# The mLSTM cell and leaky-ReLU feed-forward kernel: a written order for the first chunk and w_in in five requests per quarter

## The chip, the cores and the metric

The kernel runs on one core of a Trainium2 chip. The core has a matrix engine (TensorE, "PE" in the profile, with "PEld" for its weight loads), VectorE (DVE), ScalarE (ACT), GpSimd (POOL) and SyncE (SP), each with an instruction queue of its own, and 16 DMA engines that move data between HBM and the on-chip memory of 128 partitions. Most transfers are issued from SP's queue (SPq), a few from ScalarE's (ACTq). The metric is the device time of one execution in microseconds (us); less is better. One further execution was taken with the hardware profiler.

## What is computed

Four sequences, eight heads, 768 tokens, head dimension 40 go through an mLSTM cell; the result, 3,072 tokens by 320, goes through a two-layer feed-forward block with 2,048 hidden units:

```python
for t in range(S):
    m_new = np.maximum(f_gate[:, :, t] + m, i_gate[:, :, t])
    f_stab = np.exp(f_gate[:, :, t] + m - m_new)
    i_stab = np.exp(i_gate[:, :, t] - m_new)
    C = f_stab * C + i_stab * outer(v[t], k[t])        # per batch and head, 40 x 40
    n = f_stab * n + i_stab * k[t]
    y[t] = sigmoid(o_gate[t]) * (C @ q[t]) / max(|n . q[t]|, 1)
x = y.transpose(0, 2, 1, 3).reshape(B * S, H * D)      # 3072 x 320
h = x @ w_in                                           # w_in is 320 x 2048
out = np.maximum(0.01 * h, h) @ w_out                  # w_out is 2048 x 320
```

q, k, v and the gates arrive as 32-bit floats. The two weight matrices arrive as 64-bit floats, 5.2 MB each, and are narrowed to 32 bits on the chip.

## The kernel before, in words

The 768 tokens are cut into six chunks of 128. One *step* is one chunk of one sequence, so there are 24 steps, four to a chunk, numbered s = 4 x chunk + sequence. The recurrence is computed in the parallel form: scores of k and q, a decay matrix, and a state carried from one half chunk of 64 tokens to the next. One *group* g of the feed-forward block takes the four steps of chunk g: 512 tokens.

Up to the end of group 0 everything is issued by `first_chunk`, which walks through a text called ORDER. Each entry is a short name with numbers and calls one function. For TensorE, VectorE, ScalarE and GpSimd that text is the order in the engine's queue (`manual_schedule`); in the kernel before, SP is not among these engines, and its requests are placed by the scheduler. After it, a planned loop handles groups 1 to 5 with the remaining steps woven in.

The entries that matter here:

- `ld s i`, `lo s`: load k, q or v (i = 0, 1, 2) of a step of chunk 0, or its o gate; 128 partitions, eight rows of 160 bytes each. `fd s` loads k and v of a later step and spreads its gate decays over the partitions. `fi c` loads the gates of chunk c.
- `lw n half`: one half of quarter n of w_in (n below 4), or w_out piece n - 4 (two blocks of 128 rows). It lands in a raw 64-bit area.
- `nw n`: one of seven steps of narrowing. The first is on ScalarE (L263), six more on VectorE (L265 to L280). They need the whole of quarter n.
- `ff n`: unit n of group 0. Units 0 to 15 compute h for half of the tokens and two blocks of 128 hidden units (L918, 20 matmul instructions), and end in the leaky ReLU on ScalarE (L926); units 4 to 7 need quarter 1, 8 to 11 quarter 2, 12 to 15 quarter 3. Units 16 to 31 are the product with w_out (L953).
- `us`, `qs`, `tq`: transposes of k and q of a step of chunk 1 on TensorE. `qs` scales q by its decay, and `tq` (split_qs, L562 and L564) transposes the scaled q: 16 matmuls of 64 rows by 40 columns, into two banks, and two copies to SBUF on ScalarE.
- `up`, `upl`, `ux`: scores and states of a step of chunk 1, its outputs, and the transposes that make its x. `st`, `stc`: the first states, from chunk 0.

Partition p of either half of w_in holds the five rows 5p to 5p + 4. The lower 64 partitions (r = 0) hold 256 columns of the quarter, and the upper 64 (r = 1) the next 256. TensorE uses the two halves of its rows at the same time. A quarter comes in two requests, one for each half of the partitions (L231 to L235). The functions that the change touches, and what calls them:

Of the kernel before, what the change touches and what calls it, by code (L numbers as in the profile page):

```python
# [22 lines left out]
def kernel(  # L23
# [56 lines left out]
    psc = ctx.enter_context(tc.tile_pool(name="psc", bufs=4, space=PSUM))  # L80
# [5 lines left out]

    RG = P // BH
# [4 lines left out]
    for r in range(RG):  # L92
        nc.scalar.dma_start(f0[ts(r, BH), :], f_all[:, :P])
        nc.sync.dma_start(i0[ts(r, BH), :], i_all[:, :P])
    fi = {}

    def load_fi(c):
        t = fi[c] = wk.tile([BH, 2, P], F32, name="fi")
        eng = nc.scalar if c < 3 else nc.sync
        eng.dma_start(t[:, 0, :], f_all[:, ts(c, P)])  # L100
        eng.dma_start(t[:, 1, :], i_all[:, ts(c, P)])

    load_fi(1)
    load_fi(2)

    ident = consts.tile([P, P], F32, name="ident")
    make_identity(nc, ident[:])
    zeros = consts.tile([P, 1], F32, name="zeros")
    nc.vector.memset(zeros[:], 0.0)
# [3 lines left out]
    nc.gpsimd.memset(cmask[:], 0.0)  # L113
    nc.gpsimd.affine_select(
        cmask[:], cmask[:], compare_op=ALU.is_ge, fill=-1e30,
        base=0, pattern=[[1, P]], channel_multiplier=-1,
    )
    ident_b = consts.tile([P, P], BF16, name="ident_b")
    nc.vector.tensor_copy(ident_b[:], ident[:])
# [16 lines left out]
    for n in range(NL):  # L136
        nc.vector.memset(kn[:, n, :, D:], 0.0)
        nc.vector.memset(qn[:, n, :, D:], 0.0)
        nc.gpsimd.memset(S_t[n][:, 1, :, D:], 2.0)
        nc.gpsimd.memset(S_t[n][SL:, 0], 0.0)  # L140
# [66 lines left out]
    def load_weights(n, half=None):  # L207
# [22 lines left out]
        if n < QN:  # L230
            src = moe_w_in[:, n * QC : (n + 1) * QC].rearrange("(p k) (r c) -> r p k c", p=DP, r=2)  # L231
            for r in range(2) if half is None else (half,):
                nc.sync.dma_start(
                    to[DP * r : DP * (r + 1), :].rearrange("p (k c) -> p k c", k=KC), src[r],
                )  # L235
        else:
            rows = moe_w_out[2 * m * P : 2 * (m + 1) * P, :]
            nc.sync.dma_start(to.rearrange("p (a d) -> p a d", d=Dm), rows.rearrange("(a p) d -> p a d", p=P))
# [102 lines left out]
    def gates_T(c, bu):  # L341
        tg = psc.tile([P, 5, BH], F32, name="tg", tag="c")
# [18 lines left out]
    def load(s, i=None):  # L361
# [5 lines left out]
        if c == 0:  # L367
            d["va"] = S_t[n][:, 1]
            parts = [(d["k"][:, :, :D], k), (d["q"][:, :, :D], q), (d["va"][:, :, :D], v)]
            for dst, src in parts if i is None else parts[i : i + 1]:  # L370
                nc.sync.dma_start(dst, src[b, :, rows, :].rearrange("h p d -> p h d"))
            return
        nc.sync.dma_start(d["k"][:, :, :D], k[b, :, rows, :].rearrange("h p d -> p h d"))
        w = cw.tile([P, H, P], F32, name="w", bufs=NL)
        flat = w[:].rearrange("p h t -> p (h t)")
        d["w"] = flat[:, : H * SL].rearrange("p (h t) -> p h t", t=SL)
        if c == 1:
            for u in range(2):
                for i in range(2):
                    nc.sync.dma_start(  # L380
                        S_v[n][ts(u, SL), u, :, i, :DB],
                        v[b, :, c * P + u * SL : c * P + (u + 1) * SL, DB * i : DB * (i + 1)].rearrange("h p d -> p h d"),
                    )
            return
        d["vn"] = flat[:, H * SL : H * (SL + D)].rearrange("p (h d) -> p h d", d=D)
        nc.sync.dma_start(d["vn"], v[b, :, rows, :].rearrange("h p d -> p h d"))
# [9 lines left out]
    def load_o(s, eng=None):  # L396
# [3 lines left out]
        (eng or nc.sync).dma_start(  # L400
# [8 lines left out]
    def load_late(s, i):  # L409

        if B <= s < 2 * B:
            if i > 0:
                c, b = divmod(s, B)
                nc.sync.dma_start(natural(s, i), (k, q, o_gate)[i][b, :, ts(c, P), :].rearrange("h p d -> p h d"))
        elif s < NS:
            load_blocks(s, i)

    def load_blocks(s, i):
# [3 lines left out]
        for n in range(2):  # L422
            for r in range(2):
# [6 lines left out]
                nc.sync.dma_start(  # L430
# [7 lines left out]
    def spread(s):  # L438
# [3 lines left out]
        for u in range(2):  # L442
            nc.sync.dma_start(d["w"][ts(u, SL)], a_dr[c, 0, u, b * H : (b + 1) * H, :].partition_broadcast(SL))

    def spread_q(s):
# [4 lines left out]
        for r in range(2):  # L450
            nc.sync.dma_start(
# [23 lines left out]
    def exp_first(s, g):  # L475

        ab, n = st["ab", s - s % 2], s % 2
        if g == 0:
            st[s]["w"] = cw.tile([P, H, P], F32, name="w", bufs=NL)
# [77 lines left out]
    def split_qs(s):  # L557

        tq = [psc.tile([P, H, SL], F32, name=f"tq{u}", tag="c") for u in range(2)]
        for h in range(H):  # L560
            for u, toks, rows in subs(s):
                nc.tensor.matmul(tq[u][rows, h, :], lhsT=st[s]["qs"][toks, h], rhs=ident[toks, toks], start=True, stop=True)  # L562
        for u, toks, rows in subs(s):
            nc.scalar.copy(mixed(s)[rows, u], tq[u][rows])  # L564

    def u_split(s):
# [4 lines left out]
        bank = [psc.tile([P, H, SL], F32, name=f"tk{r}", tag="c") for r in range(2)]  # L571
# [12 lines left out]
    def u_transpose(s, i):  # L584
# [3 lines left out]
        tp = d["tp", i] = psc.tile([P, PR, P], F32, name="tkq", tag="c")  # L588
# [10 lines left out]
    def u_scores(s):  # L599
        d = st[s]  # L600
        kqT = d["kqT"]
        sc = d["sc"] = [psc.tile([P, PR, P], F32, name=f"sc{r}", tag="c") for r in range(2)]
# [12 lines left out]
    def state(s):  # L615
        c, b = divmod(s, B)
        d = st[s]
        dC = d["dC"] = psc.tile([P, PR, 2, V1], F32, name="dC", tag="c")
# [28 lines left out]
    def u_parts(s):  # L647
# [4 lines left out]
        bank = [psc.tile([P, H, SL], F32, name=f"sd{r}", tag="c") for r in range(2)]  # L652
# [27 lines left out]
    def u_values(s):  # L680
        d = st[s]
        pa = d["pa"] = psc.tile([P, H, D1], F32, name="pa", tag="c")
# [32 lines left out]
    def u_plain(s):  # L715
# [4 lines left out]
        hN = psc.tile([P, H, 2, V1], F32, name="hN", tag="c")  # L720
# [22 lines left out]
    def u_mix(s):  # L743
# [4 lines left out]
        pT = psc.tile([P, PR * P], F32, name="pT", tag="c")  # L748
# [27 lines left out]
    def gather_x(s):  # L776
# [6 lines left out]
        for r in range(2):  # L783
            nc.sync.dma_start(xT[DP * r : DP * (r + 1), b, :], src)
# [49 lines left out]
    def three_units(g, lead):  # L834
# [14 lines left out]
        def triple(j):  # L849
# [9 lines left out]
            def third():  # L859
                pe.extend(psc.tile([P, GT], F32, name=f"pe{r}", tag="c") for r in range(2))  # L860
# [20 lines left out]
    def u_x(s):  # L881
# [3 lines left out]
        xt = st["xt", s] = psc.tile([P, KF + 1, P], F32, name="xt", tag="c")  # L885
# [199 lines left out]

    ORDER = """
warm 12; g 0; ld 0 0; mk 0; ab 0; ge 0; ld 0 1; ld 1 0; lo 1; ld 0 2; ld 1 1; ld 2 0; ug 0; exp 0 0
ld 1 2; exp 1 0; exp 1 2; exp 0 2; exp 0 3; tr 0 0; tc 0 0 0; tr 0 1; exp 0 1; tr 1 0; tc 0 1 0
exp 1 3; ld 2 1; tr 1 1; sc 0; lw 0 0; scm 0 0; lw 0 1; tc 1 0 0; scm 0 1; mk 2; ab 2; lo 0; tc 1 1 0
ld 3 0; g 1; ld 3 1; ld 3 2; sc 1; exp 1 1; scm 1 1; ld 2 2; exp 2 0; tr 2 0; tr 2 1; tc 2 1 0; lw 1 0  # L1090
lw 1 1; vu 0; exp 2 2; val 0; fi 3; exp 3 0; lo 2; exp 3 2; st 0; scm 1 0; stc 0 0 0; exp 2 3
stc 0 1 0; den 0; exp 2 1; lo 3; tc 2 0 1; sc 2; o 1; lw 2 0; o 0; scm 2 0; gate 0; gp 0; ge 1
scm 2 1; nw 0; val 1; den 1; x 0; xc 0 1; gate 1; tr 3 0; tr 3 1; tc 3 1 1; nw 0; nw 0; gp 1; x 1
tc 3 0 0; sc 3; xc 1 1; vu 3; nw 0; nw 0; st 3; vu 2; vu 1; val 2; exp 3 1; exp 3 3; stc 3 1 1; st 2
stc 2 1 1; scm 3 1; scm 3 0; val 3; nw 0; tiles; ps 3; stc 2 0 1; stc 3 0 1; nw 0; o 2; den 2; den 3
gate 2; o 3; gate 3; nw 1; st 1; nw 1; nw 1; ug 1; ff 0; gp 2; x 2; xc 2 1; gp 3; nw 1; nw 1; x 3
xc 3 1; ff 1; nw 1; ff 2; nw 1; ps 0; g 2; lw 2 1; nw 2; ff 3; lw 3 0; lw 3 1; ps 2; ff 4; ff 5; nw 2
nw 2; ff 6; nw 2; ff 7; fd 4; lw 4; lw 5; stc 1 0 1; ps 1; vu 4; nw 2; nw 2; nw 2; nw 3; nw 3; nw 3
nw 3; nw 3; nw 3; nw 3; nw 4; ff 8; ff 9; ff 10; nw 4; ff 11; ff 12; nw 4; nw 4; ff 13; nw 4; nw 4
nw 4; stc 1 1 0; pm 4; sn 4 0; fd 5; ll 5 1; nw 5; ll 4 1; us 4; lw 6; lw 7; fd 6; lz 6; vu 6; fd 7  # L1100
qs 5; qs 4; pm 6; us 5; lw 8; nw 5; nw 5; nw 5; nw 5; nw 5; ff 14; pm 5; nw 5; ll 5 2; lw 9; nw 6
nw 6; lz 7; nw 6; lz 4; ex 4 3; nw 6; ff 15; ll 6 0; ex 4 3; ex 4 2; nw 6; ll 4 2; nw 6; ge 2; nw 6
pm 7; nw 7; ex 6 3; ex 6 3; tq 4; sn 5 0; nw 7; ll 7 0; ll 7 1; vu 5; up 4; nw 7; ff 16; ff 17; ex 7 3
ff 18; ff 19; nw 7; ll 8 0; nw 7; nw 7; nw 7; nw 8; nw 8; nw 8; nw 8; ug2 2; nw 8; nw 8; tq 5; upl 4
lw 10; nw 8; vu 7; ll 6 1; nw 9; nw 9; nw 9; lw 11; lz 5; fd 8; ex 7 3; nw 9; ll 9 0; nw 9; ex 5 3
nw 9; sn 6 0; nw 9; ex 5 3; ff 20; nw 10; nw 10; qs 6; ex 5 2; up 5; us 7; qs 7; nw 10; nw 10; ff 21
sn 7 0; ff 22; ux 4; upl 5; ll 9 1; nw 10; nw 10; nw 10; nw 11; nw 11; nw 11; ex 6 2; ff 23; pv 8
sq 9; nw 11; ll 7 2; nw 11; tq 7; us 6; ll 8 1; pm 8; lz 8; ex 8 3; tq 6; ff 24; nw 11; nw 11; xb0
ll 6 2; up 6; ex 7 2; up 7; ff 25; upl 6; fd 9; sn 9 0; upl 7; kq 9; fd 10; pv 9; sq 8; ll 8 2; pm 9
kq 8; ll 11 1; sq 11; fd 11; ll 10 1; sn 8 0; ll 9 2; ex 8 3; ll 11 0; lz 9; vu 8; vu 9; ff 26; ff 27  # L1110
ff 28; ff 29; ux 5; ux 6; ux 7; sq 10; ff 30; ex 8 2; ff 31; ex 9 3; ex 9 3; ll 10 0; ex 9 2
"""

    def first_chunk():

        ffs, narrow = [], {}

# [167 lines left out]
```

## Time and profile before

| | us |
|---|---|
| median of three runs | 491.97 |
| the three runs | 485.73, 491.97, 492.03 |
| the profiled execution | 488.21 |
| its span, first to last instruction | 486.4 |
| TensorE busy | 476.2 (98%) |
| VectorE busy | 357.5 (73%) |
| ScalarE busy | 194.8 (40%) |
| GpSimd busy | 158.6 (33%) |
| mean granted TensorE clock | 0.988 |
| data moved | 63.41 MB in 142,187 packets |

The page cuts the span into 40 slices of 12.2 us; a digit is the busy share in tenths. TensorE shows 8 or 9 everywhere, and DMA 7 to 9 in the first nine slices and 5 or more in most of the next fifteen. A busy TensorE is not one at its peak. The first 133 us are the first chunk; the rest is the loop. In the answers of the trace a line of the timeline is start, duration, engine, line, operation, output and inputs, count, and in brackets how long the engine was idle before it and what ended that.

### The profile page before, as it was taken

How to read it: one execution, taken by the hardware profiler on the slowest of the kernel's cores; microseconds unless marked ns; L12 is line 12 of the kernel's file. 1: busy time of each engine (PE TensorE's matmuls, PEld its weight loads, DVE VectorE, ACT ScalarE, POOL GpSimd, SP SyncE). 2: the span in 40 equal slices, each digit the busy share in tenths (PEclk: the TensorE clock that was granted, in tenths of full speed). 3: DMA queues.
4: the chain of work that ended last, by engine and by line, in shares of the span. 5: the costliest groups of instructions: out<-in, count | busy, mean ns of one | idle time of the engine just before them, and what ended most of it. 6: DMA issues, size and time to landing. Idle time of an engine off the chain costs nothing.

```text
span 486.4 us, 12790 instructions
## 1 busy us (share of the span) xinstructions
PE 476.2 (98%) x5145; PEld 378.6 (78%) x5145; DVE 357.5 (73%) x581; ACT 194.8 (40%) x509; POOL 158.6 (33%) x207
## 2 busy tenths in 40 slices
PE   8899999899999999999999999999999999999997
PEld 7788887677746489965559985558998899988997
DVE  3887788978926999677898878679899968335611
ACT  3766549554442240414251131425024642156310
POOL 4074342443401816636370654544210002000020
PEclk9979999999999999999999999999999999999999
DMA  8999878775545577776776767754151030100001
GB/s 147 194 206 164 210 180 207 166 167 114 143 138 100 143 158 215 170 179 162 156 190 183 173 156 185 192 135 139 43 230 42 1 108 1 42 16 1 0 1 55
DMA packets 142187, 63.41 MB, mean 130 GB/s; under 512 B 110320, under 2 KB 130352, under 8 KB 142128
## 3 DMA queue, kind: packets, MB, share of 16 engines
q1 hardware_dynamic: 141744, 62.47, 54.3%
q8 instruction: 40, 0.66, 0.5%
q10 hardware_dynamic: 384, 0.13, 0.1%
q14 instruction: 19, 0.16, 0.1%
HBM read 51.68 MB, written 8.27 MB: 123 GB/s over the span
## 4 chain that ended last, share of the span: by engine, by line
PE 90%; DVE 3%; ACT 3%; issue 1%; POOL 1%; POOLq 0%; DVEq 0%
PE po L994 32%; PE ph L918 28%; PE ph L844 8%; PE po L953 5%; PE pe L844 4%; PE pT L754 3%; PE sd L661 3%; PE warm L339 1%; PE pa L684 1%; PE sd L666 1%; ACT w L483 1%; DVE qn L671 1%; PE hN L724 1%; PE tk L576 1%; ACT kqT L582 1%
## 5 line engine op out<-in xcount | busy, mean ns | idle before, releaser
L918 PE MATMUL ph<-xT,w_in 64*128 64x512 f32 (+1 forms) x800 | 144.0, 513 | 0.1
L918 PEld LDWEIGHTS ph<-xT,w_in 64*128 64x128 f32 x800 | 77.9, 190 | 56.7 <-issue 51.3
L994 PE MATMUL po<-w_out,acts 128*128 128x160 f32 x640 | 91.0, 301 | 0.0
L994 PEld LDWEIGHTS po<-w_out,acts 128*128 128x128 f32 x640 | 87.5, 190 | 3.4 <-ACT w L500 1.5
L926 ACT ACTIVATE acts<-ph 128x512 f32<-128x512 f32 (+1 forms) x80 | 37.4, 508 | 89.6 <-PE ph L918 89.1
L641 POOL TENSOR_TENSOR S<-S,f 40x336 f32<-40x336 f32 x36 | 32.5, 903 | 83.4 <-PE pT L754 53.1
L500 ACT ACTIVATE w<-w,gT 128x64 f32<-128x64 f32 x160 | 41.7, 339 | 27.8 <-POOL w L492 27.8
L994 PE MATMUL po<-raw,acts 128*128 128x160 f32 x320 | 45.1, 300 | 0.0
L994 PEld LDWEIGHTS po<-raw,acts 128*128 128x128 f32 x320 | 44.0, 190 | 0.0
L1027 POOL TENSOR_TENSOR y<-y,raw 128x160 f32<-128x160 f32 x10 | 5.5, 555 | 112.0 <-ACT y L1026 112.0
L671 DVE TENSOR_TENSOR qn<-w,sd 64x512 f32<-64x512 f32 x40 | 27.3, 683 | 18.6 <-PE sd L666 12.1
L953 PE MATMUL po<-w_out,acts 128*128 128x320 f32 x128 | 38.2, 454 | 0.0
L866 DVE SCALAR_TENSOR_TENSOR acts<-ph,acts 128x512 f32<-128x512 f32 x32 | 20.6, 685 | 20.6 <-ACT acts L864 20.6
L492 POOL TENSOR_TENSOR w<-w,i 128x512 f32<-128x512 f32 x20 | 32.8, 1644 | 6.9 <-DMA w<-a_dr 3.6
L553 DVE TENSOR_TENSOR qn<-kqT,late 64x512 f32<-64x512 f32 x32 | 34.0, 1062 | 1.0
L953 PEld LDWEIGHTS po<-w_out,acts 128*128 128x128 f32 x128 | 24.7, 198 | 10.0 <-issue 1.2
L768 POOL TENSOR_TENSOR xb<-xb,den 128x320 f32<-128x320 f32 x16 | 11.6, 727 | 48.9 <-DVE xb L765 48.9
L864 ACT ACTIVATE acts<-pe 128x512 f32<-128x512 f32 x32 | 17.4, 594 | 19.1 <-PE pe L844 19.0
L772 DVE STREAM_TRANSPOSE x<-xb 128x512 f32<-128x512 f32 x16 | 17.7, 1107 | 8.0 <-POOL xb L768 8.0
L661 PEld LDWEIGHTS sd<-kqT 40*64 40x64 f32 x640 | 19.6, 135 | 4.6 <-issue 4.2
L870 ACT ACTIVATE acts<-acts 128x512 f32<-128x512 f32 x32 | 19.7, 633 | 8.0 <-DVE acts L866 8.0
L994 PE MATMUL po<-raw 128*128 128x160 f32 x160 | 22.7, 300 | 0.0
(171 smaller groups left out, 768.0 us busy)
## 6 DMA issues: line engine op xcount, KB each, us to landing
w<-a_dr SPq DMA_DIRECT2D x40, 128.0 KB, 3.6
rb<-in_k_dram SPq DMA_DIRECT2D x64, 80.0 KB, 2.7
rb<-in_q_dram SPq DMA_DIRECT2D x64, 80.0 KB, 2.5
rb<-in_o_gate_dram SPq DMA_DIRECT2D x64, 80.0 KB, 2.4
xT<-x_dr SPq DMA_DIRECT2D x32, 160.0 KB, 3.2
late<-a_dr SPq DMA_DIRECT2D x32, 128.0 KB, 3.2
x_dr<-x SPq DMA_DIRECT2D x16, 256.0 KB, 2.8
kn<-in_k_dram SPq DMA_DIRECT2D x24, 160.0 KB, 4.1
```

The costliest lines, as they stand in the source:

```text
L492: nc.gpsimd.tensor_tensor(w, w, cm2.unsqueeze(1).to_broadcast([P, H, SL]), op=ALU.add)
L500: yield nc.scalar.activation(w[:, h, :], w[:, h, :], AF.Exp, bias=gT[c][:, 0, bh : bh + 1], scale=1.0)
L553: nc.vector.tensor_tensor(mixed(s)[rows, 1 - r], d["kqT"][rows, 1].rearrange("p (h t) -> p h t", t=SL), d["ea"][rows], op=ALU.mult,)
L641: nc.gpsimd.tensor_tensor(new, old, g, op=ALU.mult)
L661: nc.tensor.matmul(bank[1 - u][toks, h, :], lhsT=kqT[rows, 0, ts(h, SL)], rhs=kqT[rows, 1, ts(h, SL)], start=True, stop=True,)
L671: nc.vector.tensor_tensor(mixed(s)[toks, u], w[toks], bank[1 - u][toks], op=ALU.mult)
L844: nc.tensor.matmul(ph[r][:], lhsT=parts["w", key][n][part, at : at + P], rhs=xs[key][part, slot, :], start=start and slot == 0, stop=stop ...
L866: nc.vector.scalar_tensor_tensor(fs[r], in0=ph[r][:], scalar=1.0 + EPS, in1=fs[r], op0=ALU.mult, op1=ALU.add,)
L918: nc.tensor.matmul(ph[r][:, cols], lhsT=w_row(r, slot, j), rhs=xT[DP * r : DP * (r + 1), slot, bs, :], start=(slot == 0), stop=(slot == KC ...
L926: nc.scalar.activation(acts[:, f, cols], ph[r][:, cols], AF.Prelu, alpha=0.01)
L953: nc.tensor.matmul(po[n][:], lhsT=acts[:, f, ts(n, P)], rhs=w_out[:, f, :], start=(f == 0), stop=(f == NF - 1),)
L994: nc.tensor.matmul(bank[:], lhsT=left[:, f, :], rhs=right[:, f, :], start=f == 0, stop=f == KH - 1)
```

## The change

Four things are changed, all of them up to the end of the first chunk.

1. ORDER is another text, and SP is now among the engines whose queue follows it. The set-up work (gate loads, identity, masks, memsets) has become entries of it, and each load names its queue with a last number (1: ScalarE's, 0: SP's). `fd` is split into `fk`, `fv` and `fs`, and `lv` loads a piece of w_out.
2. The four rotating PSUM banks of the first chunk become four banks by number, dealt out in the order of a string, BANKS; the loop opens a rotating pool of four as before.
3. `split_qs` transposes the scaled q of two steps, s and s + 1, in one call: 32 matmuls on the four quarters of the array. `tq 4` and `tq 6` replace `tq 4` to `tq 7`.
4. w_in is loaded in five requests per quarter. Request k brings row 5p + k to each partition p, for both halves r at once: 128 partitions with 2 kB each. The columns of r = 1 now lie 1,024 columns (8 kB) behind those of r = 0 instead of 256. The blocks of w_out are loaded in the order that fits this. `lw n 0` stands for k = 0, 1, 2 and `lw n 1` for k = 3, 4.

```diff
-    psc = ctx.enter_context(tc.tile_pool(name="psc", bufs=4, space=PSUM))
+    banks_stack = ctx.enter_context(ExitStack())
+    psc = banks_stack.enter_context(tc.tile_pool(name="psc", bufs=1, space=PSUM))
...
+    def bank_of(shape, name):
+        if later:
+            return later[0].tile(shape, F32, name=name, tag="c")
+        return psc.tile(shape, F32, name=name, tag=f"c{banks.pop(0)}")
...
-    def load_weights(n, half=None):
+    def load_weights(n, half=None, on=0):
...
-            src = moe_w_in[:, n * QC : (n + 1) * QC].rearrange("(p k) (r c) -> r p k c", p=DP, r=2)
-            for r in range(2) if half is None else (half,):
-                nc.sync.dma_start(
-                    to[DP * r : DP * (r + 1), :].rearrange("p (k c) -> p k c", k=KC), src[r],
-                )
+            src = moe_w_in.rearrange("(p k) (r n c) -> n k r p c", p=DP, r=2, n=QN)[n]
+            for k in range(3) if half == 0 else range(3, KC):
+                queue(on).dma_start(to.rearrange("p (k c) -> k p c", k=KC)[k], src[k])
         else:
-            rows = moe_w_out[2 * m * P : 2 * (m + 1) * P, :]
+            f = NF // 2 * (m % 2) + 2 * (m // 2)
+            rows = moe_w_out[f * P : (f + 2) * P, :]
...
     def split_qs(s):
-        tq = [psc.tile([P, H, SL], F32, name=f"tq{u}", tag="c") for u in range(2)]
+        tq = [bank_of([P, H, SL], f"tq{u}") for u in range(2)]
+        at = [(n, u, toks, rows, rows if n == 0 else slice(SL * u, SL * u + D)) for n in range(2) for u, toks, rows in subs(s)]
         for h in range(H):
-            for u, toks, rows in subs(s):
-                nc.tensor.matmul(tq[u][rows, h, :], lhsT=st[s]["qs"][toks, h], rhs=ident[toks, toks], start=True, stop=True)
-        for u, toks, rows in subs(s):
-            nc.scalar.copy(mixed(s)[rows, u], tq[u][rows])
+            for n, u, toks, rows, to in at:
+                nc.tensor.matmul(tq[u][to, h, :], lhsT=st[s + n]["qs"][toks, h], rhs=ident[toks, toks], start=True, stop=True)
+        for n, u, toks, rows, to in at:
+            nc.scalar.copy(mixed(s + n)[rows, u], tq[u][to])
...
     ORDER = """
...
+mf 1 1; ld 1 0 0; mi 0 0; zr; warm 12; mf 0 1; zk 0; mk 0; zk 2; zk 3; lw 0 0 0; lw 0 1 0; zs 2; zs 3
...
+vu 2; ld 3 2 0; exp 3 2; sc 3; lw 1 0 0; exp 3 3; scm 3 0; scm 3 1; lo 2 0; vu 3; val 2; ge 1; x 1
+st 0; val 3; st 2; nw 0; ps 2; xc 0 1; lw 1 1 0; xc 1 1; nw 0; fi 2 0; o 3; st 1; stc 1 0 0; gate 3
+stc 0 1 1; fk 4 0; stc 0 0 1; o 2; den 3; gp 3; gate 2; ff 0; den 2; lw 2 0 0; gp 2; lw 2 1 0
+stc 1 1 1; ll 4 1 0; ug 1; fs 4 0; x 3; lw 3 0 0; lw 3 1 0; st 3; stc 3 0 1; xc 3 0; ll 6 0 0; fk 7 0
+lz 7; nw 1; nw 1; nw 1; nw 1; nw 1; pm 4; x 2; nw 1; nw 1; xc 2 1; vu 4; fk 5 0; lz 5; fs 5 0; ff 1
+ff 2; ff 3; nw 2; nw 2; nw 2; lz 4; nw 2; nw 2; stc 3 1 0; lv 5 0; nw 2; nw 2; lv 4 0; ll 5 1 0; us 4
+stc 2 0 1; fk 6 0; stc 2 1 0; ff 4; ff 5; ff 6; ff 7; nw 3; nw 3; nw 3; nw 3; nw 3; nw 3; ll 4 2 0
+fs 7 0; ff 8; nw 3; qs 4; ps 1; ff 9; ff 10; ex 4 3; qs 5; vu 6; nw 4; lv 6 0; nw 5; nw 5; ll 6 1 0
...
     with tc.manual_schedule(engines={E.PE, E.DVE, E.Activation, E.Pool}):
-        first_chunk()
+        with tc.manual_schedule(engines={E.SP}):
+            first_chunk()
+        banks_stack.close()
+        later.append(ctx.enter_context(tc.tile_pool(name="psl", bufs=4, space=PSUM)))
```

More of the change, by code (lines that the diff above doesn't have):

```diff
@@ L84 @@
     cw = cells_stack.enter_context(tc.tile_pool(name="cw", bufs=2))
+    banks = []
+    later = []
+    def bank_of(shape, name):
+        if later:
+            return later[0].tile(shape, F32, name=name, tag="c")
+        return psc.tile(shape, F32, name=name, tag=f"c{banks.pop(0)}")
     RG = P // BH
@@ L135, with set_ident, set_ident_b, set_zeros @@
     acts_l = acts[:].rearrange("p f t -> p (f t)")
-    for n in range(NL):
+    def set_ident():
+        make_identity(nc, ident[:])
+    def set_ident_b():
+        nc.vector.tensor_copy(ident_b[:], ident[:])
+    def set_zeros():
+        nc.vector.memset(zeros[:], 0.0)
+    def set_mask():
+        nc.gpsimd.memset(cmask[:], 0.0)
+        nc.gpsimd.affine_select(
+            cmask[:], cmask[:], compare_op=ALU.is_ge, fill=-1e30,
+            base=0, pattern=[[1, P]], channel_multiplier=-1,
+        )
+    def set_rows(n):
         nc.vector.memset(kn[:, n, :, D:], 0.0)
         nc.vector.memset(qn[:, n, :, D:], 0.0)
+    def set_state(n):
         nc.gpsimd.memset(S_t[n][:, 1, :, D:], 2.0)
@@ L359, with load @@
     st = {}
-    def load(s, i=None):
+    def load(s, i=None, on=0):
         c, b = divmod(s, B)
@@ L370, in load @@
             for dst, src in parts if i is None else parts[i : i + 1]:
-                nc.sync.dma_start(dst, src[b, :, rows, :].rearrange("h p d -> p h d"))
+                queue(on).dma_start(dst, src[b, :, rows, :].rearrange("h p d -> p h d"))
             return
[L373 to L376, printed above, removed]
+        if i in (None, 0):
+            queue(on).dma_start(d["k"][:, :, :D], k[b, :, rows, :].rearrange("h p d -> p h d"))
+            w = cw.tile([P, H, P], F32, name="w", bufs=NL)
+            flat = d["flat"] = w[:].rearrange("p h t -> p (h t)")
+            d["w"] = flat[:, : H * SL].rearrange("p (h t) -> p h t", t=SL)
+        if i == 0:
+            return
         if c == 1:
@@ L436, in raw_blocks, with spread @@
         return blocks(rb_t[s % NR][:, i, QW : QW + RL])[:, :, :w]
-    def spread(s):
+    def spread(s, on=0):
         c, b = divmod(s, B)
@@ L570, in u_split @@
         src = (d["k"], natural(s, 1))
-        bank = [psc.tile([P, H, SL], F32, name=f"tk{r}", tag="c") for r in range(2)]
+        bank = [bank_of([P, H, SL], f"tk{r}") for r in range(2)]
         for h in range(H):
@@ L601, in u_scores @@
         kqT = d["kqT"]
-        sc = d["sc"] = [psc.tile([P, PR, P], F32, name=f"sc{r}", tag="c") for r in range(2)]
+        sc = d["sc"] = [bank_of([P, PR, P], f"sc{r}") for r in range(2)]
         for j in range(PR):
@@ L651, in u_parts @@
         run(lazy.pop(s))
-        bank = [psc.tile([P, H, SL], F32, name=f"sd{r}", tag="c") for r in range(2)]
+        bank = [bank_of([P, H, SL], f"sd{r}") for r in range(2)]
         ends = 2 if c + 1 < NB else 1
@@ L859, in third @@
             def third():
-                pe.extend(psc.tile([P, GT], F32, name=f"pe{r}", tag="c") for r in range(2))
+                pe.extend(bank_of([P, GT], f"pe{r}") for r in range(2))
                 rows(j, pe, "dif", True, True)
@@ L1116, in first_chunk @@
         ffs, narrow = [], {}
+        banks.extend(map(int, BANKS))
         def ff(n):
@@ L1128, in first_chunk @@
         acts_of = {
-            "ld": load, "lo": load_o, "loa": lambda s: load_o(s, nc.scalar), "lw": load_weights, "g": gates, "ge": gates_exp, "warm": warm,
+            "ld": load, "lo": load_o, "mf": load_f0, "mi": load_i0, "id": set_ident, "ib": set_ident_b, "zr": set_zeros, "cm": set_mask,
+            "zk": set_rows, "zs": set_state, "lw": load_weights, "lv": lambda n, on: load_weights(n, None, on), "g": gates, "ge": gates_exp, "warm": warm,
             "ug": lambda c: gates_T(c, bus[c][0] if c == 0 else bus.pop(c)[0]),
@@ L1134, in first_chunk @@
             "gp": gate_scale, "nw": step, "ps": prepare_step, "x": u_x, "xc": x_copy, "ff": ff,
-            "warmer": warmer, "idle": idle, "fd": feed, "ll": load_late,
+            "warmer": warmer, "idle": idle, "fk": lambda s, on: load(s, 0, on), "fv": lambda s, on: load(s, 1, on), "fs": spread, "ll": load_late,
             "pm": prep_mask, "us": u_split, "lz": begin, "ex": lambda s, n: run(lazy[s], n), "qs": prep_qs, "kq": prep_kq,
```

117 lines of the change are left out of this document (53 added, 64 removed).

## The prediction

> **What bounds the kernel now.** I read the busy slices and the chain first. TensorE is busy 476.2 of 486.4 us and the chain that ended last is 90% TensorE. From 133.2 us on its timeline is one unbroken run of group matmuls, which the change does not touch. So only the first 133.2 us can move, and there TensorE idles 7.0 us in all (the windows of 10 us up to 130 add to 123.0 busy of 130).
>
> Next, the windows of the opening. The columns are the stretch, its length, busy time of TensorE, weight loads, VectorE, ScalarE and GpSimd with counts, the granted clock, the DMA share and GB/s:
>
> ```profile
> 10.00:20.00 10.00, 9.20 (x122) 7.49 (x121) 7.12 (x16) 7.96 (x30) 0.70 (x2) 1.00 1.10 190
> 20.00:30.00 10.00, 8.49 (x97) 7.43 (x99) 8.82 (x19) 7.89 (x20) 6.46 (x10) 1.00 1.06 202
> 30.00:40.00 10.00, 10.00 (x83) 8.55 (x85) 9.50 (x18) 3.86 (x9) 6.31 (x14) 0.66 1.12 209
> 40.00:50.00 10.00, 9.89 (x88) 8.51 (x90) 7.17 (x13) 7.21 (x17) 1.82 (x5) 1.00 0.82 144
> ```
>
> All 16 DMA engines are full here, yet move only 190 to 209 GB/s, and w_in is most of it. The list of DMA issues and ScalarE's timeline show what that costs:
>
> ```profile
> acts<-in_moe_w_in_dram SPq DMA_DIRECT2D x4, 640.0 KB, 8.0
> raw<-in_moe_w_in_dram SPq DMA_DIRECT2D x4, 640.0 KB, 11.6
> ```
>
> ```profile
> 56.79 1.36 ACT L263 ACTIVATE late<-raw 128x1280 bf16<-128x1280 bf16 x1
> ```
>
> The first two lines are the eight w_in requests (median us from issue to landing). The last is the first conversion step of the last quarter, nw 3. By the packet records the quarters' packets run from 11.2 to 18.6, 22.8 to 29.4 and, for two quarters, 30.9 to 44.8 us. The last quarter is thus in place 12 us before nw 3 starts, and none of the four steps L263 on w_in waits for a DMA; VectorE's queue of conversions decides when they start. From nw 3 to the end of the first chunk takes 133.2 - 56.8 = 76.4 us.
>
> **The change, part by part.** *Joint q transposes.* Two calls replace four of 1.03 to 1.09 us (L562 groups), with twice the matmuls on disjoint quarters of the array: 2.1 us of TensorE gone. The eight copies at L564 (0.58 us each) stay.
>
> *New order and fixed banks.* The TensorE work of the chunk is otherwise the same, the twelve warm-up matmuls (5.49 us) included. The 7.0 us of idle time are the ceiling of a gain; I take half, 3.5 us, with 0 and 7 as ends. Banks dealt by hand can at worst return that. The memsets that now stand in the order are the same ones (0.06 to 0.5 us each), beside the warm-up.
>
> *SP's queue.* Every transfer is now issued in the written order, so a request that waits holds all behind it. In particular the k load of step 4 (fk 4), which waits for step 0's state matmuls, stands ahead of quarters 2 and 3 of w_in.
>
> *The w_in requests.* Eight requests of 640 KB become twenty of 256 KB; the packets stay 2 kB, 2,560 in all. Before, one request reaches 64 partitions, and most of its packets take 150 to 190 ns (median 166). The shortest seventh take 81 to 90 ns, and w_out's 2,560-byte packets, whose requests span 128 partitions, take 102 ns (median). A quarter's 640 packets in 6.5 us are 201 GB/s. So engines share a path two by two in a half-partition request, and one path carries 25 GB/s, or 80 ns per packet. The new shape removes that. SBUF — State Buffer in the Trainium skill (section "Door 1: The DMA port swizzle") says that partitions 0 to 63 reach only eight of sixteen ports, measured there at 196 GB/s; the trace's 201 agrees, and by this page alone w_in would need half its time.
>
> But how many engines take a request? The trace shows only one answer: 459 requests end in 7,344 packets of 4 bytes (one more is odd), sixteen each, from 16 KB to 640 KB. The cut is therefore made by an index and not by size, and every one of these requests has, on both sides, an outermost dimension that 16 divides (128, 64, 32 or 16). The new source is written r, p, c: its outermost dimension is the partition half r, with two entries 8 kB apart. The rows p lie 80 kB apart, so the two cannot be merged into one run of 128. No row shows such a request. The bounds: sixteen engines, 2,560 x 80 ns / 16 = 12.8 us for all of w_in; or two engines, one per half, always the same two, 1,280 x 80 ns = 102.4 us. I take the second: all rows have a cut along the outermost index, and this one has two entries. Both ends are kept below. DMA: Bandwidth & Descriptors in the Trainium skill (section "Why a DMA increments its semaphore by 16 and not by 1") says the same: the number of engines is the largest up to 16 that divides the slowest dimension of both sides, and the lowest-numbered ones are used. No run so far shows it; by this page the sum is the one below, by the other page alone it is that of the first rival.
>
> **The sum.** One request puts 64 packets on each of the two engines, 5.1 us; a quarter takes 25.6 us. Every other SP request has a sixteenth of its packets on these two engines, behind what was issued earlier, and is complete only then: a q, k, v or o load of 1,024 packets of 160 bytes (14 ns, median) has 64 there, 0.9 us.
>
> - Quarter 0: ahead of it SP issues four gate loads (1.79 us in all before) and five step loads (0.4 to 0.9 us each), whose data need 4.5 us; its packets start near 9 us, end near 35 and have landed near 36. Before, step nw 0 on ScalarE ran at 21.7.
> - Behind it stand eleven loads (v of step 1, all of steps 2 and 3, the o gates): 9.9 us. Steps 1 to 3 thus wait until 37 to 45 us for data that they had by 25 to 34.
> - Quarter 1 ends near 71. Then fk 4 (its wait is over by then: step 0's matmuls need only quarter-free data and come near 50) and quarter 2, near 98; one q load and the spread of step 4, 1.5 us; quarter 3 near 125.
>
> In the new order nw 3's first step stands on ScalarE after unit ff 7 and ahead of every later leaky ReLU. TensorE can run ff 8 and ff 9 into its four banks and then stops. From 125 us on remain: the step itself, 1.4; ff 10 to 15, six at 2.25 = 13.5; ff 16 to 31, 128 matmuls at 0.275 = 35.2; three splits of k and q at 1.0; two joint transposes at 1.05; four each of scores (1.05), outputs (1.14) and x transposes (0.55); the gates, 0.75. That is 1.4 + 65.5 us. To it I add 3 us for the clock (the trace has it at 0.50 for 6.8 and 3.4 us in this chunk, 5.1 us lost, and here TensorE restarts after waits of 10 us and more) and 3 us for waits on VectorE, which has some 57 us of work in the same stretch (nw 3 at 6.3, eight w_out conversions at 3.6, and the steps). Together 73 us, beside 76.4 for the stretch that began at the same step before. The chunk ends at 198 instead of 133.2: 65 us later.
>
> 486.4 + 65 = 551.4 us of span. The profiled execution was 488.21, 1.8 above its span: 553.2. The median of the runs is 491.97, 3.8 above that execution: **557 us**, 13% slower. Ends: at 76 or 90 ns a packet quarter 3 comes 5 us earlier or 13 later; the stretch after it takes 66 (TensorE alone) to 84 us. With 0 to 4 us between execution and median that gives 541 to 585; I give 530 to 590.
>
> **The rivals.** *Sixteen engines share each request* (not slower). For it: no request of the trace ran on fewer. Then w_in needs 12.8 us instead of the 27.9 us of its three bursts and the o loads no longer hold ScalarE (3.1 us in all), but w_in was no wait before: what is gained is the order and the transposes, 3.5 + 2.1, so 480.8 of span, 482.6, and 486 by the median (479 to 492).
>
> *Two engines per request, but another pair each time.* Then up to eight requests run side by side, a quarter lands some 7 us after its issue as before, and the time is again near 486 to 490. Against it: nothing in the trace tells the pairs apart.
>
> *SP's fixed line, with sixteen engines* (slower). Quarters 2 and 3 wait behind fk 4. That is free as long as step 0's state matmuls end before 45 us (they ran by 33.9 before); beyond, each us late is one us late at nw 3. At 58 us it would be 13 us: 505.
>
> **Chances.** Forecast 0.80; sixteen engines 0.14; changing pairs 0.03; SP's line 0.03. Two per cent, about what a measurement of this kernel can tell from no change, is 482.1 to 501.8. Of the first rival a third of its range is under that: faster 0.05; same 0.09 + 0.03 = 0.12; slower 0.80 + 0.03 = 0.83. The range leaves out the three rivals, 0.20 in all, which is as much as it may.
>
> **What would show it.** The twenty w_in requests take 15 us and more to land; the DMA share between 10 and 125 us falls from about 1 to under 0.3; the 4-byte packets are fewer than sixteen per request; L263 of w_in waits for DMA at about 36, 71, 98 and 125 us; TensorE idles for tens of us and its granted clock falls with it; the stretch from nw 3 to the first group's matmuls is 70 to 76 us. With packets on all engines at 80 to 100 ns and no wait at L263, the forecast is wrong in its first step. If the two engines are right and the time is not, then nw 3 was not the gate, or the packet time was not 80 ns.

## The result and the profile after

| | before | after |
|---|---|---|
| median, us | 489.15 (4 runs, 485.73 to 492.03) | 554.27 (4 runs, 553.98 to 555.15) |
| profiled execution, us | 488.21 | 554.53 |
| its span, us | 486.4 | 552.7 |
| TensorE busy, us | 476.2 | 491.7 |
| mean granted TensorE clock | 0.988 | 0.926 |

The ratio is 1.1345, with a 95% interval of 1.1295 to 1.1395: 13% slower. The page of the kernel after, with the busy slices (13.8 us each) of TensorE, its clock and the DMA engines:

```profile
span 552.7 us, 12808 instructions
...
PE   7439850847999999999999999999999999999997
...
PEclk8855775686999999999999999999999999999999
DMA  4162212127867766476676768686425103010001
```

All that is new lies in the first ten slices: TensorE has holes there, and the DMA engines, which showed 7 to 9 tenths in the first slices of before, mostly show 1 and 2. Windows of the same kernel, with the columns of the windows shown of before (granted clock, DMA share and GB/s last):

```profile
20.00:30.00 10.00, 1.02 (x10) 0.90 (x9) 0.00 (x0) 0.00 (x0) 0.00 (x0) 0.68 0.21 65
30.00:40.00 10.00, 3.00 (x14) 2.63 (x14) 3.98 (x11) 4.24 (x12) 0.00 (x0) 0.50 0.67 129
40.00:50.00 10.00, 9.96 (x60) 8.73 (x59) 4.52 (x13) 6.11 (x20) 3.29 (x7) 0.50 0.37 81
80.00:90.00 10.00, 0.96 (x10) 0.45 (x6) 0.00 (x0) 0.77 (x2) 0.00 (x0) 0.76 0.14 51
126.10:199.00 72.90, 69.04 (x970) 54.36 (x970) 64.37 (x104) 42.21 (x106) 28.74 (x35) 0.95 0.78 184
```

From 20 to 30 us and from 80 to 90 us almost nothing computes (TensorE is busy for 1 us of each 10) and the DMA share is 0.14 to 0.21; two engines of sixteen would be 0.125. The packet records say the same: w_in's 2 kB packets have a median of 84 ns (166 before), and 24.5 of them end per microsecond while quarters 1 to 3 arrive (23.7 for quarter 0). That is two engines at 82 ns each. The packets of 4 bytes are 7,257 instead of 7,345: 451 x 16 + 20 x 2 + 1, which is two for each of the twenty w_in requests. ScalarE's timeline has the first narrowing step of each quarter:

```profile
35.08 1.33 ACT L286 ACTIVATE late<-acts 128x1280 bf16<-128x1280 bf16 x1 [17.51 <-DMA acts<-in_moe_w_in_dram]
71.47 1.33 ACT L286 ACTIVATE late<-acts 128x1280 bf16<-128x1280 bf16 x1 [7.00 <-DMA acts<-in_moe_w_in_dram]
98.74 1.35 ACT L286 ACTIVATE late<-raw 128x1280 bf16<-128x1280 bf16 x1 [17.60 <-DMA raw<-in_moe_w_in_dram]
126.07 1.33 ACT L286 ACTIVATE late<-raw 128x1280 bf16<-128x1280 bf16 x1 [13.14 <-DMA raw<-in_moe_w_in_dram]
```

Before, none of the four waited for a DMA; now all do. The first chunk ends where TensorE's timeline has the first matmuls of group 1. Before:

```profile
133.10 13.15 PE L918 MATMUL ph<-xT,w_in 64*128 64x512 f32 x60
```

After, with the restart behind the last quarter ahead of it:

```profile
127.73 7.26 PE L945 MATMUL ph<-xT,w_in 64*128 64x256 f32 x40 [11.17 <-ACT acts L953]
...
199.21 13.14 PE L945 MATMUL ph<-xT,w_in 64*128 64x512 f32 x60
```

133.1 to 199.2 is 66.1 us, and the spans differ by 66.3. TensorE's longest waits up to there are these (total, times, longest):

```profile
PE tk L603 <- DMA rb<-in_q_dram: 18.3, 1, 18.3
PE tkq L617 <- DMA kn<-in_k_dram: 15.4, 1, 15.4
PE ph L945 <- ACT acts L953: 11.2, 1, 11.2
PE ph L945 <- ACT xT L927: 6.3, 1, 6.3
```

Two of the four are not for w_in: they are for k and q loads that stand behind it. SP's timeline (start, duration of the whole row, requests) shows how:

```profile
6.08 14.89 SPq L257 DMA_DIRECT2D acts<-in_moe_w_in_dram  x5
21.01 5.06 SPq L394 DMA_DIRECT2D S<-in_v_dram  x1
26.12 5.09 SPq L116 DMA_DIRECT2D fi<-in_f_gate_dram  x1
```

A load that took SP 0.4 to 0.9 us to issue took 5.1 here, which is the time of one w_in request on two engines (64 packets x 82 ns = 5.2). That fits SP itself standing still until those two have worked off a request; in any case what is written behind it in SP's queue is not even issued in that time.

### The profile page after: what moved, and what is told of

It is laid out like the page before. It is cut to its first block, busy times and chain, and to the rows that moved or that the text cites. A ratio compares the mean times of both kernels' runs of the same rounds, so it can differ in the third digit from the quotient of the medians.

```text
span 552.7 us, 12808 instructions
## 1 busy us (share of the span) xinstructions
PE 491.7 (89%) x5145; PEld 391.3 (71%) x5145; DVE 360.3 (65%) x582; ACT 194.5 (35%) x508; POOL 152.4 (28%) x207
## 4 chain that ended last, share of the span: by engine, by line
PE 75%; SPq 13%; DMA 7%; ACT 2%; DVE 1%; issue 1%; POOL 1%; POOLq 0%; ACTq 0%
PE po L1021 28%; PE ph L945 22%; PE ph L871 7%; SPq L257 6%; DMA rb<-in_q_dram 5%; PE pe L871 3%; PE po L980 3%; PE pT L781 3%; PE sd L688 2%; PE pa L711 2%; SPq L394 1%; SPq L397 1%; SPq L406 1%; SPq L116 1%; PE sc L633 1%
## 5 line engine op out<-in xcount | busy, mean ns | idle before, releaser
L945 PE MATMUL ph<-xT,w_in 64*128 64x512 f32 (+1 forms) x800 | 151.6, 533 | 17.4 <-ACT acts L953 11.2
L945 PEld LDWEIGHTS ph<-xT,w_in 64*128 64x128 f32 x800 | 83.6, 201 | 75.7 <-issue 51.2
L518 POOL TENSOR_TENSOR w<-w,i 128x512 f32<-128x512 f32 x20 | 31.6, 1583 | 36.8 <-DMA w<-a_dr 36.6
L288 DVE TENSOR_SCALAR late<-late 128x1280 bf16<-128x1280 bf16 (+1 forms) x8 | 5.1, 641 | 48.9 <-ACT late L286 48.8
L980 PE MATMUL po<-w_out,acts 128*128 128x320 f32 x128 | 36.5, 438 | 0.0
L980 PEld LDWEIGHTS po<-w_out,acts 128*128 128x128 f32 x128 | 23.7, 190 | 9.3
L795 POOL TENSOR_TENSOR xb<-xb,den 128x320 f32<-128x320 f32 x16 | 11.6, 727 | 48.6 <-DVE xb L792 48.6
## 6 DMA issues: line engine op xcount, KB each, us to landing
w<-a_dr SPq DMA_DIRECT2D x40, 128.0 KB
late<-a_dr SPq DMA_DIRECT2D x32, 128.0 KB
```

The source lines that it names most:

```text
L518: nc.gpsimd.tensor_tensor(w, w, cm2.unsqueeze(1).to_broadcast([P, H, SL]), op=ALU.add)
L945: nc.tensor.matmul(ph[r][:, cols], lhsT=w_row(r, slot, j), rhs=xT[DP * r : DP * (r + 1), slot, bs, :], start=(slot == 0), stop=(slot == KC ...
L980: nc.tensor.matmul(po[n][:], lhsT=acts[:, f, ts(n, P)], rhs=w_out[:, f, :], start=(f == 0), stop=(f == NF - 1),)
```

## The experiments

Unless a line says otherwise, a ratio is to the kernel before, run on the same chip, and edits are to the kernel after.

**One part undone: the requests.** w_in in two requests per quarter again, all else as after (the 8 kB spacing and w_out's block order too):

```diff
-            src = moe_w_in.rearrange("(p k) (r n c) -> n k r p c", p=DP, r=2, n=QN)[n]
-            for k in range(3) if half == 0 else range(3, KC):
-                queue(on).dma_start(to.rearrange("p (k c) -> k p c", k=KC)[k], src[k])
+            src = moe_w_in.rearrange("(p k) (r n c) -> n r p k c", p=DP, r=2, n=QN)[n]
+            queue(on).dma_start(
+                to[DP * half : DP * (half + 1), :].rearrange("p (k c) -> p k c", k=KC), src[half],
+            )
```

> The changed kernel with one thing undone: w_in comes again in two requests per quarter, one for each half of the partitions (64 partitions of five rows of 2 kB); the columns of the halves stay 8 kB apart, and the written order, the fixed banks and the joint transposes stay. Theory A, two DMA engines per request because the outermost dimension of the source has two entries: all of the loss goes, 478 to 492 us, and a quarter's packets run over 6.5 to 7.5 us at about 166 ns each, as before the change. Theory B, the written order of SP's queue holds the loads back: still over 540 us. Theory C, packets of columns 8 kB apart are slow: still over 540 us.

Measured: 482.26 us, ratio 0.9872 (0.9824 to 0.9921), span 481.3; 7,345 packets of 4 bytes, w_in's at 165 to 168 ns. The narrowing steps begin at 15.59, 38.27, 45.82 and 56.55 us, with no wait for a DMA. From TensorE's timeline:

```profile
128.04 13.14 PE L946 MATMUL ph<-xT,w_in 64*128 64x512 f32 x60
```

The five requests alone thus cost 72 us (554.27 against 482.26), and the rest of the change gains 1.3%. By its median this kernel is the fastest of all that ran; the next one is within the spread of its runs.

**The same five requests, on all engines.** Only the order of the source's dimensions changes, so that 64 rows p and not two halves r are outermost:

```diff
-            src = moe_w_in.rearrange("(p k) (r n c) -> n k r p c", p=DP, r=2, n=QN)[n]
+            src = moe_w_in.rearrange("(p k) (r n c) -> n k p r c", p=DP, r=2, n=QN)[n]
```

> The changed kernel with the source of the five requests written p, r, c instead of r, p, c: the same twenty requests, the same 128 partitions, the same 2,560 packets of 2 kB from the same addresses, but an outermost dimension of 64 entries instead of two. It leaves out the placing of the halves: row p of both halves lies in partitions 2p and 2p + 1, so h is computed from exchanged weights; the work on every engine is the same. Theory A: sixteen engines take each request, a quarter's packets run over 3.2 to 4.5 us at 80 to 110 ns, and the time is 478 to 490 us. Theory C, that such requests of one row per partition and 8 kB between the columns are slow in themselves, and theory B, that the written order does it: both over 540 us.

Measured: 483.13 us, ratio 0.9877 (0.9821 to 0.9932), span 481.2. The packets of 4 bytes are 7,537 = 471 x 16 + 1, sixteen per request; w_in's packets have a median of 84 ns. From the list of DMA issues (KB each, median us to landing):

```profile
acts<-in_moe_w_in_dram SPq DMA_DIRECT2D x10, 256.0 KB, 4.2
raw<-in_moe_w_in_dram SPq DMA_DIRECT2D x10, 256.0 KB, 5.0
```

Same count, size, spacing and packets, and 71 us less: what costs is the outermost index. This kernel leaves out the placing of the halves and computes h from exchanged weights, so it shows the price of the index and is no repair. A quarter took 5.2 to 6.7 us of packets, and not the 3.2 to 4.5 expected; the records show other loads between w_in's. More to the point, packets that take half the time brought nothing over the halves (483.13 against 482.26): the narrowing steps start at 15.63, 40.74, 48.30 and 58.50 us, no earlier than there, and none waits for a DMA.

**One part alone: the requests in the old order.** To the kernel before, only the five requests and w_out's block order:

```diff
-            src = moe_w_in[:, n * QC : (n + 1) * QC].rearrange("(p k) (r c) -> r p k c", p=DP, r=2)
...
+            src = moe_w_in.rearrange("(p k) (r n c) -> n k r p c", p=DP, r=2, n=QN)[n]
+            for k in range(3) if half == 0 else range(3, KC):
+                nc.sync.dma_start(to.rearrange("p (k c) -> k p c", k=KC)[k], src[k])
...
```

> The kernel before with the five requests per quarter alone (and the blocks of w_out in the order that fits them); order, banks, transposes and the scheduler's placing of SP's requests as before. Theory A: the four quarters need 102 us on two engines whatever the order, so last quarter near 120 to 130 us and 545 to 575 us in all; the 4-byte packets are sixteen per request but two for each of the twenty. Theory B: within 2% of the kernel before.

Measured: 563.76 us, ratio 1.1543 (1.1487 to 1.16), 7,257 packets of 4 bytes. The last quarter's first step on ScalarE:

```profile
126.51 1.34 ACT L262 ACTIVATE late<-raw 128x1280 bf16<-128x1280 bf16 x1 [13.95 <-DMA raw<-in_moe_w_in_dram]
```

It starts within 0.5 us of where it does in the kernel after, under another order and another way of placing SP's requests: two engines set that moment. The chunk then ends at 210.8 instead of 199.2, so the rest of the change is worth 11.6 us of the chunk (9.5 us between the medians) once w_in is this late.

**Ten requests of one half each.** Each of the five cut by r, so that one partition dimension of 64 is left outermost.

> The changed kernel with each of the five requests per quarter cut in two by r: ten requests of 64 partitions with one row of 2 kB each, r = 0 and r = 1 by turns. Theory A: sixteen engines again, four packets each, a request 4 x 160 ns long when two engines share a path; SP issues forty requests instead of twenty, at 0.4 to 0.6 us each, beside the other work; 480 to 494 us. Theory C, requests of one row per partition are slow: over 540 us. If it is 2% or more above the run with two requests per quarter, the number of requests on SP's queue costs something by itself.

Measured: 485.04 us, ratio 0.9919 (0.9886 to 0.9951), with 7,857 = 491 x 16 + 1 packets of 4 bytes: sixteen per request. Twice as many requests as after, and not slower than before. So the number of requests is not the cause; nor is the 8 kB distance within a request, which the kernel with 64 rows outermost has too.

**The joint transposes alone**, in the kernel before, at the place of the second call of each pair:

> The kernel before with the joint transposes alone: two calls, at the places of the second call of each pair. The working by rows gave 2.1 us less work on TensorE; if TensorE's queue carries that through, the ratio is 0.996. If the gain of the run with undone requests (482.3 against 488.7 us) comes from the transposes, the ratio is near 0.987; if they are hidden behind VectorE, 1.000.

Measured: ratio 0.9974 (0.9938 to 1.0011). From TensorE's timeline, a joint call and the next user of its copies:

```profile
83.68 1.10 PE L563 MATMUL tq<-ident,y 64*40 64x64 f32 x64
...
113.42 0.33 PE L662 MATMUL sd<-kqT 40*64 40x64 f32 x2 [1.30 <-ACT qn L565]
```

64 instructions take what 32 took (1.03 to 1.09 us), as the sum had it. But in the old order the four copies of a pair come together, and the scores behind them wait 1.3 us. Between nothing and 2.1 us gained this run can't decide.

**Is it the largest divisor up to sixteen?** In the kernel with halves, quarter 3's halves are cut into requests of 40 and 24 partitions (one execution):

> As the run with two requests per quarter, but each half of quarter 3 comes in two requests, of 40 and of 24 partitions. Theory A, that a request is cut over the largest number of engines up to sixteen that divides its outermost dimension on both sides: 10 engines for 40 and 12 for 24, so 457 x 16 + 2 x 10 + 2 x 12 + 1 = 7,357 packets of 4 bytes. If every request with at least sixteen entries is cut over sixteen engines: 461 x 16 + 1 = 7,377. Time within 1% of that run.

Measured: 7,357 packets of 4 bytes = 457 x 16 + 2 x 10 + 2 x 12 + 1, the count by the rule to the packet; 7,377 would have been a cut that fills all engines. The time is 485.06 us, 0.6% above that run. The count shows 10 and 12 only as their sum, 22 for each half. With that, and with 2 and 16 counted above, the rule of the Trainium skill (DMA: Bandwidth & Descriptors, "Why a DMA increments its semaphore by 16 and not by 1") holds here: as many engines as the largest number up to sixteen that divides the outermost dimension of both sides.

**One quarter on two engines.** In the kernel with halves, only quarter 3, then only quarter 0, comes in the five requests.

> As the run with two requests per quarter, but quarter 3 alone comes in the five requests over both halves (source r, p, c). Theory A with the gate at nw 3: the quarter's 25.6 us on two engines start when those of quarter 2 are through, near 44 us, and end near 70 us; nw 3 ran at 56.6 us, so 13 us later, of which units ff 8 to 11 cover little: 491 to 498 us. If two slow engines were only slow for the loads behind them and not for the gate: within 1% of 482 us.

> As the run with two requests per quarter, but quarter 0 alone comes in the five requests over both halves. Theory A: it lands near 35 instead of 15 us, and the step loads behind it with it, so ScalarE and VectorE stand for 20 us at nw 0; nothing later makes that up: 496 to 506 us. If the later queue of conversions has slack: less than 490 us.

Quarter 3 alone: 495.98 us, ratio 1.0132 (1.0083 to 1.0182). Its first step on ScalarE:

```profile
69.21 1.33 ACT L292 ACTIVATE late<-raw 128x1280 bf16<-128x1280 bf16 x1 [12.47 <-DMA raw<-in_moe_w_in_dram]
```

12.7 us later than 56.55, and the chunk ends 13.2 us later (141.3): as expected, a late quarter 3 is paid one to one.

Quarter 0 alone: 510.34 us, ratio 1.0424 (1.0381 to 1.0467), above the 496 to 506 expected. Quarter 0 begins to be narrowed at 35.80, 20.2 us later, but the chunk ends at 154.9, 26.9 later. The 6.7 us more are lost here (TensorE's timeline, from step 2's k transposes to `ff 0`):

```profile
37.17 1.08 PE L623 MATMUL tkq<-ident,kn 128*128 128x128 f32 x4 [14.59 <-DMA kn<-in_k_dram]
...
39.69 3.48 PE L717 MATMUL pa<-S,w 128*128 128x41 f32 x16
...
59.61 4.58 PE L951 MATMUL ph<-xT,w_in 64*128 64x256 f32 x20
```

The stretch takes 22.4 us; with halves it takes 12.9 (19.19 to 32.12), and its `pa` groups 1.88 to 1.98 us. The window of it says why TensorE is full and yet slow:

```profile
37.00:59.60 22.60, 21.87 (x150) 19.64 (x150) 11.88 (x24) 12.87 (x39) 4.54 (x10) 0.50 0.86 157
```

It is busy for 97% of it at a granted clock of 0.50. Is the clock the cause, or only what shows a starved TensorE? That asks for a kernel in which TensorE does not stop while it waits for k.

**TensorE kept busy.** To the kernel with a late quarter 0, useless identity matmuls ahead of step 2's k transposes, into the bank that these then overwrite; N = 32, 64 and 84 calls:

```diff
+        if s == 2 and i == 0:
+            for _ in range(N):
+                nc.tensor.matmul(tp[:, 0, :], lhsT=ident[:], rhs=ident[:], start=True, stop=True)
```

> As the run with quarter 0 alone in five requests (510.3 us), with 32 matmuls of the identity with itself added ahead of step 2's k transposes, where TensorE waits 14.6 us for that step's data: they fill the wait and change no result. Theory H, that the stall costs more than its length because the granted clock falls to 0.50 in it and stays there for 41 us of small matmuls (the stretch from those transposes to unit ff 0 takes 22.4 us instead of 12.9): with the wait filled the clock stays at 1.00, the stretch takes 13 to 15 us, and the time is 499 to 504 us. If the stretch is long because of late data, the added matmuls change nothing: 509 to 512 us.

> The kernel of e8_first (quarter 0 of w_in in five requests, the other quarters in halves) with 64 calls of identity matmuls, 128 instructions on TensorE, instead of the 32 of e9_kept_busy, at the same place: ahead of step 2's k transposes. e9's filler took 7.39 us and ended at 28.4 us; 9.0 us of TensorE's wait for step 2's k were left open, and its clock fell to 0.50 at 33.7 us. Twice as many take some 14.8 us and end near 36, where that wait ended, so TensorE no longer stands still there. Theory H (the extra 6.7 us of e8 are lost because TensorE waits, its granted clock falls to 0.50, and the small matmuls of steps 2 and 3 and of the opening's other work then run at half speed): the clock stays at 1.00 from 37 to 60 us, the stretch from step 2's k transposes to ff 0 takes 13 to 15 us instead of 22.4, the chunk ends near 147, and the time is 499 to 504 us. Rival (the extra comes from the late k and v loads and from what they push on ScalarE and VectorE, the clock only shows it): the stretch stays at 20 us or more and the time at 508 to 513, whatever the clock does.

> The kernel of e10_filled with 84 calls of identity matmuls, 168 instructions, instead of 64 calls. e10's filler took 14.54 us and ended at 33.9 us; a wait of 3.4 us for step 2's k was left, and in it the clock fell again, at 36.0 us, to 0.50 until 63.3 us; the stretch from step 2's k transposes to ff 0 took 22.3 us, so neither theory was told apart. With 84 calls the filler takes 14.54 x 84 / 64 = 19.1 us and ends near 38.5, 1.1 us after that wait ended, so TensorE goes from it into step 2 without a stop. Theory H (the extra of e8 is lost to the granted clock, which a stop of TensorE lowers and which the small matmuls that follow do not bring back): the clock stays at 1.00 from 36 to 60 us, the stretch takes 13 to 15 us, ff 0 starts near 52 instead of 59.6, and the time is 499 to 504 us. Rival (the late k, v and w_in and what they push on ScalarE and VectorE set the stretch): the clock is at 1.00, but the stretch still takes 20 us or more, with waits of TensorE in it, and the time is 509 to 513. If the clock falls although TensorE never stops, the stop is not what lowers it, and H stands on the clock alone.

| calls | filler ends, us | stop left, us | clock at 0.50, us | k transposes to `ff 0`, us | chunk ends | median, us | ratio |
|---|---|---|---|---|---|---|---|
| 0 | | 14.6 | 23.0 to 64.0 | 22.4 | 154.9 | 510.34 | 1.0424 (1.0381 to 1.0467) |
| 32 | 28.4 | 9.0 | 33.6 to 64.3 | 22.6 | 156.9 | 511.78 | 1.0462 (1.0431 to 1.0492) |
| 64 | 33.9 | 3.4 | 36.0 to 63.4 | 22.3 | 155.1 | 510.10 | 1.0427 (1.0314 to 1.054) |
| 84 | 38.8 | none | none | 13.2 | 147.1 | 503.28 | 1.0301 (1.0234 to 1.0367) |

With 32 and 64 calls a stop was left, the clock fell in it and nothing was told apart. From TensorE's timeline with 64 calls:

```profile
37.35 1.11 PE L626 MATMUL tkq<-ident,kn 128*128 128x128 f32 x4 [3.44 <-DMA kn<-in_k_dram]
...
39.70 3.48 PE L720 MATMUL pa<-S,w 128*128 128x41 f32 x16
```

With 84 calls (TensorE's timeline, then its window):

```profile
19.76 19.00 PE L624 MATMUL tkq<-ident 128*128 128x128 f32 x168
...
39.52 1.88 PE L720 MATMUL pa<-S,w 128*128 128x41 f32 x16
...
51.77 2.43 PE L954 MATMUL ph<-xT,w_in 64*128 64x256 f32 x20
```

```profile
37.00:51.70 14.70, 13.38 (x166) 12.24 (x165) 12.55 (x25) 12.97 (x39) 6.25 (x10) 1.00 1.10 194
```

The same work, begun 1.4 us later, ends 7.8 us earlier, and the chunk and the span (500.3 against 508.1) with it. All executions agree: their spans are 499.3 to 504.3 us here and 507.9 to 509.2 without filler. k, v and w_in are no earlier than without filler: SP issues the k and v loads held behind quarter 0 at 32.6, 37.3 and 39.9 us instead of 32.5, 37.1 and 39.7, and quarter 0's first step starts at 35.98 instead of 35.80. So the low clock is the cause of the extra loss, and here the stop is what lowered it; the last section has falls without one. What is left is the pure lateness: 147.1 against 128.0 is 19.1 us for a quarter 0 that is 20.4 us late.

## Why the prediction was right

| step | predicted | measured |
|---|---|---|
| engines per w_in request | 2, always the same | 2; 24.5 packets per us over quarters 1 to 3 |
| time per packet | 80 ns | 82 ns |
| quarters in place, first step | 36, 71, 98, 125 | 35.1, 71.5, 98.7, 126.1 |
| gate of the chunk | nw 3's first step | TensorE restarts at 127.7, 0.3 us after that step's end, behind the first leaky ReLU that follows it |
| from there to the chunk's end | 73 | 73.1 |
| chunk's end | 198 | 199.2 |
| span | 551.4 | 552.7 |
| profiled execution | 553.2 | 554.53 |
| median | 557 | 554.27 |

*The number of engines* was the whole question, and was read from what the trace of before had only indirectly: 4-byte packets that did not grow with size. The first rival (sixteen) fell by the count 7,257, the second (changing pairs) by the rate: several pairs at once would end more than 24.5 packets per us. The third, SP's fixed line, cost nothing, since with halves no narrowing step waits for a DMA.

*The 73 us after the gate* agree in their parts too: TensorE is busy 69.0 of 72.9 us, at a mean clock of 0.95, where 66.9 of work, 3 for the clock and 3 for waits had been added up. VectorE's work there came to 64.4 us instead of 57, and TensorE's idle time to 3.9 us instead of 3.

*The last 3.8 us*, from the profiled execution to the median, were a mis-sized term. They came from three runs of before that spread over 6 us; in the later comparisons, of 7 to 17 runs, its median lay at 487.3 to 489.5. The kernel after has its median 0.3 us under the profiled execution. Two smaller sums of the prediction do not come out: by its own terms the upper end is 581 us (551.4 + 13 + 11 + 1.8 + 4) and not 585, and a quarter, not a third, of the first rival's range lies under 482.1. The stated range holds either way.

*The order*, taken as half of the 7.0 us of idle time, is the term that went wrong, though rival one's span (480.8) nearly equals the 481.3 measured with halves. There the idle time did not shrink: TensorE is busy 119.5 of 128.0 us, so 8.5 idle. What shrank is its busy time, by some 6.6 us: 3.4 because less is run at half clock (1.7 us lost instead of 5.1), up to 2.1 by the joint transposes, the rest not accounted for. Quarter 3 begins to be narrowed only 0.2 us earlier than before (56.55 against 56.79), so nearly all of the 5.1 us by which the chunk is shorter come behind that point, and of the clock's 3.4 us only 1.7 do. How much of the 1.3% each edit of the order makes stays open.

*SP* was expected to issue on and its loads to complete late; in fact it was held itself. The landings are the same either way here.

*What would show it*: a DMA share under 0.3 from 10 to 125 us was too simple. It is 0.14 to 0.21 while w_in is alone and reaches 0.67 when the loads behind it are let go. The clock fell, as foretold. In the kernel after this should have cost little by itself: the stretch from step 2's k transposes to `ff 0` takes 22.5 us there too, but TensorE waited for each later quarter anyway; that is argued from the waits, not tried.

## What to carry to other kernels

Before regrouping a DMA, look at the outermost dimension of both sides as the request carries it: it decides how many engines share the request, and an index of two ahead of 64 rows turns sixteen engines into two; the 4-byte packets per request show the number. A transfer on few engines delays all that stands behind it in its queue, so the first waits to appear may be for loads that were not touched. And faster packets buy nothing where, as here, no consumer was waiting for the data.

## What the runs showed of the hardware

In the clock records of these traces TensorE's granted clock is either 1.00 or 0.50, and it changes only after whole multiples of 3.41 us, so the moments given here are no finer than that. With a late quarter 0 it fell to 0.50 once TensorE had stopped (0.4, 5.2 and 2.1 us after the stop began, with 0, 32 and 64 filler calls). It then did not come back although TensorE was 97 to 100% busy for over 20 us with matmuls of 41 to 128 columns; in these three kernels it returned 3.7 to 4.4 us after `ff 0`, the first unit of 256 columns, began (2.3 us in the kernel after). Without the stop the same small matmuls ran at 1.00 throughout. So 19 us of useless work made a kernel 7 us faster.

Neither half of this is a rule. The clock also fell without a long stop: in the kernel before at 31.4 us, though TensorE had not stood still for more than 0.7 us at a time in the 15 us ahead of it, and in the kernel with p, r, c at 28.0 us, with no stop longer than 0.35 us in the 13 us ahead. And small matmuls did bring it back once: in the kernel with quarter 0 alone in five requests it had already been at 0.50 from 9.4 to 16.2 us, and no matmul in that time had more than 128 columns.

The Trainium skill (TensorE: Matmul & The Clock Gate, "What's actually happening") has the clock halved after an idle window of some 3.4 us and full again after some 3.4 us of sustained activity; the falls in the long waits agree roughly, those without a long stop do not, and the late returns do not either: being busy by the profile was not enough here. What exactly counts as activity wasn't tried.
